# A pair's weighted sum as one group, and a shared two-bank tile, in an attention kernel with experts behind it

## The chip, the cores and the metric

The kernel runs on one core of one Trainium2 chip. The metric is the time of one execution on the device in microseconds (us); the time given for a kernel is the median of several runs. Both kernels compute the same outputs from the same inputs.

## What is computed

Causal attention with a learned decay, 4 batches of 8 heads, 576 positions of 64 features; then a layer of eight experts, of which each of the 2304 tokens uses one; then a dense layer with a squared ReLU. All in float32.

```python
scores = scale * np.matmul(q, k.transpose(0, 1, 3, 2))
cum = np.cumsum(np.maximum(s, 0.0), axis=-1)
bias = -(cum[:, :, :, None] - cum[:, :, None, :])
scores = np.where(causal, -1000000000.0, scores + np.minimum(bias, 0.0))
attn = np.exp(scores - np.max(scores, axis=-1, keepdims=True))
attn = attn / (np.sum(attn, axis=-1, keepdims=True) + 1e-09)
out = np.matmul(attn, v)                      # 32 heads of 576 x 64
x = out as 2304 tokens x 512
e_idx = np.argmax(x @ w_gate, axis=1)         # one expert a token
out[mask] = gate_w[mask, None] * eom[mask, e, None] * (relu(x[mask] @ w1[e]) @ w2[e])
return np.square(relu(out @ w_in)) @ w_out
```

## The kernel before, in words

The program has three stages: attention, which fills the first quarter of the span together with the choice of experts; the experts; the dense layer. The change lies in attention and touches the border to the experts.

Attention works on 16 **pairs** of heads, four pairs to a batch. A pair's 576 rows are four blocks of 128 and a tail of 64. Its scores come in seven **units**: 0 and 1 are the first two blocks, each with both heads; 2, 3 and 10, 11 are the third and fourth block of the first and of the second head; 4 is the **tail**, the last 64 rows of both heads, 576 columns wide and thus two PSUM banks. The order of units is `[0, 1, 3, 11, 2, 10, 4]`. Every unit goes through the same steps: `emit_s` (line 636) computes scores on TensorE into PSUM; `emit_m` (line 663, VectorE) adds the mask while it reads PSUM and finds the row's maximum; `emit_e` (line 680, ScalarE) is the exponential; `emit_t` (line 696) transposes the result p on TensorE; `emit_v` (lines 715 and 717) copies the transposes to SBUF. Then the weighted sum: `emit_pv` (line 733) multiplies with v in two **halves**, half 0 the first 256 rows (two blocks of keys), half 1 the other 320 (five blocks); `emit_ov` (line 744) copies the result out of PSUM, `emit_rc` (lines 759 to 762) makes the reciprocals of the row sums, `emit_xt` and `emit_xe` (lines 771 and 806) transpose and scale the result, and `store_x` writes it to memory.

q and k of a coming pair are transposed on TensorE too (`qk_pe`, lines 549 and 551): part 0 is q, part 1 is k, part 2 the tails of both. `qk_hi` (line 576, ScalarE) writes the high part of each, and `qk_lo` (line 580, VectorE) the rest that the high part leaves, so that scores are made of products of two parts. The first two pairs take four such products per score, the others two, with their decay terms loaded beside.

There are three sets of PSUM tiles in this stage: a ring of three one-bank tiles `s` for the scores of the units other than the tail and for `emit_xt`; a ring of three one-bank tiles `t`; and one tile `s2` of two banks for the tail's scores. The ring `t` holds the transposes of p, those of q and k, and the weighted sums (there is no ring of their own, since `O=0`), and some steps of the gate's logits. A tile is taken in turn; whoever takes it waits until the tile's earlier readers are done.

The order of the work is a sorted list. Each step is entered with a time of its own by `at(key, fn)`, in units of which a pair has seven, and the list is then written out in the order of the keys, each engine getting its steps in that order. The keys come from the table `K_`: `pv` (a half's blocks), `ov`, `rc`, `xt`, `xe`, `sx` (behind the half), `qk`, `qkh`, `qkl` (transposes, high, low), `lt` (logits). The q and k of most pairs are made one frame early (`early`):

```python
def early(pp):
    return min(NU, 3 * max(pp - ND, 0))
```

After the last pair a first piece of expert work runs, whose products are `early_h` (line 1071) and `early_y` (line 1099). `x_hi` and `x_lo` (lines 1341 and 1347) then bring the first chunk's tokens from PSUM to the tile `xt`, and `emit_h` (line 1431) starts the experts' first products with it.

## Time and profile before

| what | value |
|---|---|
| median of three runs | 861.39 us (860.45 to 861.93) |
| profiled execution, its own time | 862.74 us |
| its span | 861.0 us |
| mean granted clock of TensorE in it | 0.998 of full speed |
| TensorE busy | 843.1 us, 98% of the span |
| VectorE, ScalarE, GpSimd busy | 60%, 53%, 30% |

The time of an execution is a little longer than its span, which runs from the first to the last instruction that the profiler records. Times in rows are microseconds from the span's start. PE is TensorE's matmul, PEld its weight load, DVE is VectorE, ACT is ScalarE, POOL is GpSimd. `t<-ident,qk` is an instruction that writes tile `t` from `ident` and `qk`; a float32 matmul or transpose leaves more than one record where it needs more than one pass. In brackets stands the idle time before an instruction and what ended it.

### The profile page before, as it was taken

What the parts mean: (1) busy time and instruction counts of PE and PEld (TensorE: products, weight loads), DVE (VectorE), ACT (ScalarE), POOL (GpSimd) and SP (SyncE); (2) the same over time, 40 slices, a digit from 0 to 9 for tenths busy, and PEclk for the clock granted to TensorE, in tenths of its full rate; (3) what the DMA queues carried; (4) which work ended last, traced back from release to release, by engine and by line L of the source; (5) the groups of instructions that cost most, each with busy time, mean ns of one, the idle gap of its engine ahead of it and who ended that gap; (6) DMA issues with size and microseconds to landing.
All of it is one profiled execution on the core that took longest, in us unless ns stands there. A gap on an engine that the chain in (4) does not pass through costs nothing.

```text
span 861.0 us, 15161 instructions
## 1 busy us (share of the span) xinstructions
PE 843.1 (98%) x5412; PEld 748.7 (87%) x5412; DVE 520.4 (60%) x1180; ACT 452.3 (53%) x1012; POOL 262.1 (30%) x304
## 2 busy tenths in 40 slices
PE   8999999999999999999999999999999999999995
PEld 6876777777799999999999999999999999999994
DVE  7667777978777677768976767664233343232221
ACT  7787878988465446566655545443233232233221
POOL 6322334543126465566422232331101011001001
PEclk9999999999999999999999999999999999999999
DMA  7676677753287898999983433321010121001001
GB/s 168 137 162 142 144 183 180 178 127 91 78 278 232 255 252 266 233 280 274 296 246 96 147 120 101 100 84 62 13 62 37 37 75 38 1 1 37 1 0 40
DMA packets 113029, 113.14 MB, mean 131 GB/s; under 512 B 66034, under 2 KB 83954, under 8 KB 112947
## 3 DMA queue, kind: packets, MB, share of 16 engines
q1 hardware_dynamic: 104962, 96.68, 42.1%
q0 software_dynamic: 3664, 9.62, 3.3%
q10 hardware_dynamic: 4320, 5.80, 2.0%
q8 instruction: 45, 0.74, 0.4%
q14 instruction: 38, 0.30, 0.1%
HBM read 80.50 MB, written 23.32 MB: 121 GB/s over the span
## 4 chain that ended last, share of the span: by engine, by line
PE 47%; issue 31%; DVE 6%; ACT 6%; POOL 5%; DMA 4%; POOLq 1%; SPq 0%; ACTq 0%; DVEq 0%
PE z L1431 14%; PE z L1482 7%; PE z L1473 6%; PE s L636 5%; PE t L733 5%; PE t L696 4%; DMA cv<-in_moe_w_out_dram 2%; ACT p L680 2%; POOL out_dram L1541 1%; DVE w L250 1%; POOL cvm L1400 1%; PE t L549 1%; POOL cvm L1399 1%; ACT sta L576 1%; DMA w_out_d<-cvm 1%
## 5 line engine op out<-in xcount | busy, mean ns | idle before, releaser
L1431 PE MATMUL z<-xt,w 128*128 128x384 f32 (+6 forms) x1920 | 329.7, 320 | 0.7 <-DVE h L1442 0.6
L1431 PEld LDWEIGHTS z<-xt,w 128*128 128x128 f32 x1920 | 308.1, 188 | 9.8 <-DVE h L1442 1.2
L1482 PE MATMUL z<-w,h 128*128 128x512 f32 x864 | 214.9, 393 | 0.0
L1482 PEld LDWEIGHTS z<-w,h 128*128 128x128 f32 x864 | 160.7, 188 | 29.3
L1451 DVE SCALAR_TENSOR_TENSOR r<-z,r 128x384 f32<-128x384 f32 x96 | 53.3, 556 | 127.2 <-ACT r L1450 127.2
L1450 ACT ACTIVATE r<-z 128x384 f32<-128x384 f32 x96 | 47.2, 492 | 150.3 <-PE z L1431 149.3
L1473 PE MATMUL z<-h,w 128*128 128x304 f32 (+5 forms) x768 | 111.3, 294 | 0.4 <-DVE h L1442 0.2
L1473 PEld LDWEIGHTS z<-h,w 128*128 128x128 f32 x768 | 104.0, 189 | 1.2 <-ACT h L1441 0.4
L1399 POOL TENSOR_TENSOR cvm<-cvm,cva 128x512 f32<-128x512 f32 x32 | 43.5, 1361 | 170.6 <-DVE cva L1395 121.9
L1541 POOL DMA_INDIRECT out_dram<-ysb,tok_m x18 | 17.4, 969 | 245.5 <-ACT ysb L1528 183.2
L1458 DVE TENSOR_TENSOR h<-r,h 128x384 fp32r<-128x384 f32 x96 | 61.0, 636 | 50.3 <-ACT h L1457 49.7
L680 ACT ACTIVATE p<-p,nm 128x128 f32<-128x128 f32 (+3 forms) x144 | 84.3, 590 | 3.7 <-DVE nm L663 2.3
L1457 ACT CAST h<-r 128x384 fp32r<-128x384 f32 x96 | 49.3, 513 | 64.1 <-DVE r L1451 63.8
L250 DVE TENSOR_TENSOR w<-stg,w 128x1024 fp32r<-128x1024 f32 x49 | 75.1, 1534 | 5.4 <-ACT w L246 5.4
L663 DVE CUSTOM_DVE_ANT_0 p<-s,mask 128x128 f32<-128x128 f32 (+3 forms) x128 | 59.7, 486 | 30.4 <-PE s L636 29.3
L696 PE MATMUL t<-ident,p 128*128 128x128 f32 x400 | 69.1, 283 | 2.8 <-DVE sta L580 1.1
L246 ACT CAST w<-stg 128x1024 fp32r<-128x1024 f32 x49 | 51.4, 1049 | 22.0 <-POOL cvm L1400 18.2
L696 PEld LDWEIGHTS t<-ident,p 128*128 128x128 f32 x400 | 44.4, 140 | 18.7 <-ACT p L680 6.2
L597 POOL CAST stb<-sta 64x1152 fp32r<-64x1152 f32 x28 | 31.4, 1150 | 79.7 <-PE s L636 46.3
L1400 POOL TENSOR_TENSOR cvm<-cvs,cvm 128x512 f32<-128x512 f32 x32 | 54.2, 1694 | 2.5
L636 PE MATMUL s<-sta 128*64 128x288 f32 (+4 forms) x204 | 50.0, 342 | 0.9 <-DVE sta L580 0.9
L715 ACT COPY pt<-t 128x512 f32<-128x512 f32 (+1 forms) x94 | 47.0, 515 | 7.3 <-PE t L733 4.1
(242 smaller groups left out, 1024.8 us busy)
## 6 DMA issues: line engine op xcount, KB each, us to landing
stg<-in_moe_w_dram SPq DMA_DIRECT2D x42, 512.0 KB
cv<-in_moe_w_out_dram SPq DMA_DIRECT2D x16, 512.0 KB
stx<-in_moe_w_dram SPq DMA_DIRECT2D x14, 512.0 KB
cv<-in_moe_w_in_dram SPq DMA_DIRECT2D x14, 512.0 KB
xr<-yT_d SPq DMA_DIRECT2D x8, 768.0 KB
qk<-in_q_dram SPq DMA_DIRECT2D x32, 128.0 KB
v<-in_v_dram SPq DMA_DIRECT2D x32, 128.0 KB
stg<-in_moe_w_dram SPq DMA_DIRECT2D x16, 256.0 KB
```

What stands on the lines that cost most here:

```text
L250: nc.vector.tensor_tensor(out=lo, in0=raw.pop(job), in1=hi.bitcast(F32), op=ALU.subtract)
L636: nc.tensor.matmul(ps[0:mw, d0:d0 + nn], lhsT=ql[r, m0:m0 + mw], rhs=kl[r, c0:c0 + nn], start=(i == 0 and (tail or n == 0)), stop=(done an ...
L663: nc.vector.tensor_tensor_reduce(out=dst, in0=src, in1=msk, scale=-1.0, scalar=3.0e38, op0=ALU.add, op1=ALU.min, accum_out=nm[:, c:c + 1])
L680: nc.scalar.activation(out=pt[:, cs], in_=pt[:, cs], func=AF.Exp, scale=-1.0, bias=nm[:, c:c + 1], accum_out=rs[:, r:r + 1])
L696: nc.tensor.transpose(tp[:, i * P:(i + 1) * P], pt[:, j0:j0 + P], ident)
L1399: nc.gpsimd.tensor_tensor(out=m, in0=m, in1=a.bitcast(F32), op=ALU.mult)
L1400: nc.gpsimd.tensor_tensor(out=m, in0=sq, in1=m, op=ALU.add)
L1431: nc.tensor.matmul(ps[:, 0:n], lhsT=wa[:, zw, kk, fl * P:(fl + 1) * P], rhs=xt[:, zx, kk, 0:n], start=(i == 0), stop=(i == 3 * KD - 1))
L1451: nc.vector.scalar_tensor_tensor(out=gg, in0=ps[:, 0:TT], scalar=0.0, in1=gg, op0=ALU.max, op1=ALU.mult)
L1458: nc.vector.tensor_tensor(out=ht[:, 1], in0=gg, in1=ht[:, 0].bitcast(F32), op=ALU.subtract)
L1473: nc.tensor.matmul(y_acc[g][d][:, 0:n], lhsT=wb[:, zw, fl, d * P:(d + 1) * P], rhs=ht[:, zh, 0:n], start=(f == 0 and i == 0), stop=(f == n ...
L1482: nc.tensor.matmul(acc, lhsT=ht[:, zh, c * P:(c + 1) * P], rhs=wb[:, zw, fl, :], start=(first and i == 0), stop=(last and i == 2))
```

## The change

Five things are done together.

- The transposes of q and of k (parts 0 and 1) go into the two banks of one `s2` tile, for every pair from the third on but one (the fourth, which stays in ring `t`): thirteen pairs. Part 2 stays in ring `t`.
- The weighted sum of a pair is one group: half 0 moves to directly before half 1, both into the two banks of one `s2` tile. The last pair keeps its two groups and ring `t`.
- The transposed p of units 0 and 1 has two buffers instead of one, each laid out without a gap (768 floats a partition and pair instead of 1024), and its copies are contiguous.
- The reciprocals of both halves are made in one step.
- Keys: transposes of q and k at `qk2`, later by 0.95, 0.56 and 0.30; the rest of half 0 at `x0`; `sx` and one `lt`.

```diff
     wz=1.0,
     ring=['o', 't', 'o', 'o', 't', 's'],
     go=7.15,
-    lt=[[-0.37, -0.33, 0.07, 0.12], [-0.22, 0.14, 0.64, 0.96]],
+    lt=[[-0.37, -0.33, 0.07, 0.12], [-0.36, 0.14, 0.64, 0.96]],
     ltact=[1, 1],
     ptb=1,
     order=[0, 1, 3, 11, 2, 10, 4],
@@ -54,18 +54,20 @@
...
     sck=-5.35,
     qk=[-3.45, -2.16, -1.89],
+    qk2=[-2.5, -1.6, -1.59],
     qkh=0.61,
     qkl=0.65,
     dup=-2.9,
     dupa=0.6,
-    pv=[[3.74, 3.87], [8.47, 8.49, 8.51, 8.53, 8.57]],
+    x0=10.87,
+    pv=[[8.45, 8.46], [8.47, 8.49, 8.51, 8.53, 8.57]],
     ovact=[1, 1],
     gk=[4.59, 4.65, 5.02, 5.22, 5.65, 6.55, 7.35, 7.38, 7.54, 8.68, 9.78, 10.48, 10.95, 11.72, 12.72, 14.11, 14.46, 14.36, 14.48, 14.97, 15.87, 16.25, 17.18, 17.4, 19.12, 20.76],
...
     xe=1.32,
-    sx=2.42,
+    sx=3.9,
     w0=6.88,
     wld=2.9,
...
             cum_k = apool.tile([P, S], F32R, name="cum_k")
             cum_q = cq_p.tile([P, 2 * ND, S], F32R, tag="cq", name="cum_q")
-            pt0 = [apool.tile([P, 2, 2, 256], F32, name=f"pt0{a}") for a in range(K_["ptb"])]
+            pt0 = [apool.tile([P, 2, 3 * P], F32, name=f"pt0{a}") for a in range(2)]
             pt1 = [apool.tile([P, 2, NB, S - 256], F32, name=f"pt1{a}") for a in range(K_["ptb"])]
 
             def bank(r):
@@ -499,6 +501,8 @@
                 for _ in range(n):
                     nc.tensor.matmul(wt[:, 0:w], lhsT=onesb, rhs=onesb.unsqueeze(1).to_broadcast([P, w // P, P]), start=True, stop=True)
...
             qk_ps = {}
 
+            def early(pp):
+                return min(NU, 3 * max(pp - ND, 0))
+
+            def in_s2(pp):
+                return pp >= ND and early(pp) != 3
+
             def qk_pe(pp, part):
-                ps = qk_ps[pp, part] = bank(K_["ring"][part])
+                if part < 2 and in_s2(pp):
+                    if part == 0:
+                        qk_ps[pp] = ps_2.tile([P, 1024], F32, tag="s2", name="s2")
+                    ps = qk_ps[pp][:, 512 * part:512 * part + 512]
+                else:
+                    ps = bank(K_["ring"][part])
+                qk_ps[pp, part] = ps
                 if part < 2:
                     t = raw_q[pp][:, part * QM:(part + 1) * QM]
                     for c in range(NB - 1):
@@ -701,8 +717,8 @@
                 j0 = 0
                 for i, (tp, n) in enumerate(t_t.pop((pp, u))):
                     if u < 2:
-                        src = tp[:, 0:n * P].rearrange("p (h j i) -> p h j i", h=2, i=P)
-                        dst = pt0[pb][:, :, 0:u + 1, u * P:(u + 1) * P]
+                        src = tp[:, 0:n * P].rearrange("p (h c) -> p h c", h=2)
+                        dst = pt0[pp % 2][:, :, u * P:(2 * u + 1) * P]
                     elif u == NB - 1:
                         src = tp[:, 0:n * P].rearrange("p (j h i) -> p h j i", h=2, i=TAIL)
                         dst = pt1[pb][:, :, j0:j0 + n, S - TAIL - 256:S - 256]
@@ -721,19 +737,27 @@
             def emit_pv(pp, half, jbs):
                 vt = raw_v[pp]
                 if jbs[0] == 0:
-                    o_t[pp, half] = ps_o.tile([P, 512], F32, tag=o_tag, name=o_tag)
+                    if pp == NPAIR - 1:
+                        o_t[pp, half] = ps_o.tile([P, 512], F32, tag=o_tag, name=o_tag)
+                    else:
+                        if half == 0:
+                            o_t[pp] = ps_2.tile([P, 1024], F32, tag="s2", name="s2")
+                        o_t[pp, half] = o_t[pp][:, 512 * half:512 * half + 512]
                 o = o_t[pp, half]
                 last = 1 if half == 0 else NB - 1
-                pt = (pt0 if half == 0 else pt1)[pp % K_["ptb"]]
                 n = 256 if half == 0 else S - 256
                 base = 0 if half == 0 else 2
                 for jb in jbs:
                     c0 = max(jb - base, 0) * P
+                    if half == 0:
+                        pt = pt0[pp % 2][:, :, 2 * c0:n + c0]
+                    else:
+                        pt = pt1[pp % K_["ptb"]][:, :, jb, c0:n]
                     for hd in range(2):
                         nc.tensor.matmul(
                             o[64 * hd:64 * hd + 64, c0:n],
                             lhsT=vt[:, jb, hd, :],
-                            rhs=pt[:, hd, jb, c0:n],
+                            rhs=pt[:, hd],
                             start=(jb == 0), stop=(jb == last))
 
             def emit_ov(pp, half, act):
@@ -754,7 +778,7 @@
                 b, j = divmod(pp, HP)
                 rc = rc_t[pp] = rc_all[b % 2][:, 2 * j:2 * j + 2]
                 rsv = rs.rearrange("p (h t) -> p h t", h=2)
-                b0, b1 = (0, 2) if half == 0 else (2, NB)
+                b0, b1 = (0, 2) if half == 0 else (2 if pp == NPAIR - 1 else 0, NB)
                 if half == 1:
                     nc.vector.tensor_copy(out=rs[0:TAIL, 2 * NB - 1:2 * NB], in_=rs[P - TAIL:P, NB - 1:NB])
                 nc.vector.tensor_scalar(
@@ -1231,12 +1255,7 @@
             new_half(wpool1, (0, "a"), "w0")
             new_half(wpool1, (0, "b"), "w1")
 
-            order = K_["order"]
-            NU = len(order)
             at(NU * ND + 0.5, init_spare)
-
-            def early(pp):
...
                 base = NU * pp
@@ -1250,12 +1269,12 @@
                     else:
                         at(K_["od"][0], scale_tail, pp, nc.vector)
                     for part in range(3):
-                        tq = t0 + K_["qk"][part] - early(pp) + (0 if pp >= ND else K_["q1"])
+                        tq = t0 + K_["qk2" if in_s2(pp) else "qk"][part] - early(pp) + (0 if pp >= ND else K_["q1"])
                         at(tq, qk_pe, pp, part)
                         at(tq + K_["qkh"], qk_hi, pp, part)
                         at(tq + K_["qkl"], qk_lo, pp, part)
                 if pp >= ND:
-                    tb = t0 + max(K_["dup"], K_["qk"][2] + K_["qkl"] - early(pp) + 0.4)
+                    tb = t0 + max(K_["dup"], K_["qk2" if in_s2(pp) else "qk"][2] + K_["qkl"] - early(pp) + 0.4)
...
                     at(tb - 0.04, copy_b, pp)
...
                     tx = tv + K_["xe"]
                     at(tv + K_["ov"], emit_ov, pp, half, K_["ovact"][half])
-                    at(tv + K_["rc"], emit_rc, pp, half)
+                    if end or half == 1:
+                        at(tv + K_["rc"], emit_rc, pp, half)
+                    if not end and half == 0:
+                        tv = tv - K_["pv"][0][-1] + K_["x0"]
+                        tx = tv + K_["xe"]
                     at(tv + K_["xt"], emit_xt, pp, half)
                     if end:
                         at(tx, emit_xl, pp, half)
```

The rows below show what this moves on the engines. A row is one instruction or several alike: line, operation, what it writes and reads, its size, and the engines or DMA queues that it waits for.

TensorE behind the tail's scores of the third pair, before; the last row of the tail's scores stands first:

```order
L636 MATMUL s_865<-sta_137 64x288 x4
L549 MATMUL t<-ident,qk 128x128 [waits DMAHW3_49,DMAHW2_49,PE_49]
L549 MATMUL t<-ident,qk 128x128 x3
L733 MATMUL t<-pt_154,v_142 64x256 [waits DMAHW5_49,Activation_49]
L733 MATMUL t<-pt_154,v_142 64x256 [waits DMAHW6_49]
L733 MATMUL t<-pt_154,v_142 64x128 x2
L696 MATMUL t<-ident,p 128x128 [waits Activation_49]
L696 MATMUL t<-ident,p 128x128 x2
L636 MATMUL s<-sta_135 128x192 [waits DMAHW0_49,DVE_49,Pool_49]
L636 MATMUL s<-sta_135 128x192 [waits DMAHW7_49]
L636 MATMUL s<-stb_139 128x192 x2
L549 MATMUL t<-ident,qk 128x128 [waits DMAHW6_49,DMAHW5_49,Activation_49]
```

TensorE at the same place, changed; here `s_892` is an `s2` tile, and the tail's scores end three rows above the first row:

```order
L652 MATMUL s<-sta_135 128x192 [waits DMAHW0_49,DVE_49,Pool_49]
L652 MATMUL s<-sta_135 128x192 [waits DMAHW7_49]
L652 MATMUL s<-stb_139 128x192 [waits DMAHW5_49]
L652 MATMUL s<-stb_139 128x192 [waits DMAHW6_49]
L565 MATMUL s_892<-ident,qk 128x128 [waits DMAHW3_49,DMAHW2_49,DVE_49]
L565 MATMUL s_892<-ident,qk 128x128 x3
L795 MATMUL s<-ident,oT_310 128x128 x2
L712 MATMUL t<-ident,p 128x128 [waits Activation_49]
L712 MATMUL t<-ident,p 128x128 x2
L652 MATMUL s<-sta_135 128x256 x2
L652 MATMUL s<-stb_139 128x256 x2
L565 MATMUL s_892<-ident,qk 128x128 [waits DVE_49]
```

The weighted sum of half 0 (line 733) is gone from here; the q transposes, which were first, stand behind the scores of the next unit (192 wide), and the k transposes, which stood there, behind those of the unit after it (256 wide); both now wait for VectorE.

ScalarE from the last exponentials of the third pair on, before:

```order
L680 ACTIVATE p,rs_156<-p,nm 128x384 [waits DVE_49]
L576 ACTIVATE sta_137<-t 128x512 [waits DMAHW1_49,DMAHW0_49,PE_49]
L744 COPY oTx<-t 128x256 [waits PE_49]
L680 ACTIVATE p,rs_156<-p,nm 128x576 [waits DVE_49]
L576 ACTIVATE sta_137<-t 128x512 [waits DMAHW1_49,PE_49,Pool_49]
L715 COPY pt_155<-t 128x3x128 [waits PE_49]
L576 ACTIVATE sta_137<-t 128x2x64 [waits PE_49]
L680 ACTIVATE p,rs_157<-p,nm 128x128 [waits DVE_49,Activation_49]
L680 ACTIVATE p,rs_157<-p,nm 128x128 [waits DVE_49]
L715 COPY pt_155<-t 128x2x3x64 [waits PE_49]
L715 COPY pt_155<-t 128x2x2x64 [waits PE_49]
```

ScalarE at the same place, changed:

```order
L696 ACTIVATE p,rs_157<-p,nm 128x384 [waits DVE_49,Activation_49]
L696 ACTIVATE p,rs_157<-p,nm 128x576 [waits DVE_49]
L592 ACTIVATE sta_137<-s_892 128x512 [waits DMAHW1_49,DMAHW0_49,PE_49]
L731 COPY pt_156<-t 128x3x128 [waits PE_49]
L696 ACTIVATE p,rs_158<-p,nm 128x128 [waits DVE_49] x2
L592 ACTIVATE sta_137<-s_892 128x512 [waits DMAHW1_49,DVE_49,PE_49]
L592 ACTIVATE sta_137<-t 128x2x64 [waits PE_49]
L731 COPY pt_156<-t 128x2x3x64 [waits PE_49]
L731 COPY pt_156<-t 128x2x2x64 [waits PE_49]
L696 ACTIVATE p,rs_158<-p,nm 128x256 [waits DVE_49,Activation_49]
L696 ACTIVATE p,rs_158<-p,nm 128x256 [waits DVE_49]
```

The exponential of the tail (576 wide) moved from behind q's high part to ahead of it; the copy of a weighted sum (`oTx`) is gone from here; k's high part (the second row of 512) moved behind the copy of a transpose and two exponentials.

ScalarE at the end of attention, before, where `sta_136` holds the early expert work and `xt` the first chunk's tokens:

```order
L1088 CAST sta_136<-z_3600 128x512 [waits PE_49]
L1077 ACTIVATE qk<-z_3577 128x512 [waits PE_49]
L1088 CAST sta_136<-z_3653 128x512 [waits PE_49]
L1341 CAST xt<-z_3659 128x4x128 [waits PE_49,Activation_49,Pool_49]
L1341 CAST xt<-z_3690 128x4x96 [waits PE_49]
L1586 COPY ysb<-z_3646 128x512 [waits DMAHW5_49,DMAHW6_49,DMAHW1_49,DMAHW7_49,DMAHW0_49,PE_49]
```

ScalarE at the same place, changed:

```order
L1112 CAST sta_136<-z_3543 128x512 [waits DMAHW5_49,PE_49]
L1101 ACTIVATE qk<-z_3520 128x512 [waits PE_49]
L1112 CAST sta_136<-z_3596 128x512 [waits PE_49]
L1364 CAST xt<-z_3602 128x4x128 [waits DMAHW0_49,DVE_49,DMAHW5_49,PE_49,DMAHW7_49,Activation_49,Pool_49]
L1364 CAST xt<-z_3633 128x4x96
L1609 COPY ysb<-z_3589 128x512 [waits DMAHW6_49,DMAHW5_49,DMAHW7_49,DMAHW1_49,DMAHW0_49]
```

The first cast of `xt` has got four waits more, on VectorE and three DMA queues, the second cast has lost its own, and the copy `ysb` behind them no longer waits for TensorE.

## Rows read from the trace of the kernel before

**Rows 1.** The page's busy time, share of the span and instructions of each engine.
```profile
PE 843.1 (98%) x5412; PEld 748.7 (87%) x5412; DVE 520.4 (60%) x1180; ACT 452.3 (53%) x1012; POOL 262.1 (30%) x304
```

**Rows 2.** Windows: us, then PE, PEld, DVE, ACT, POOL busy, PEclk, DMA share, GB/s.
```profile
40.00:80.00 40.00, 38.81 (x310) 29.72 (x308) 28.24 (x99) 31.96 (x93) 10.80 (x14) 1.00 0.70 158
...
400.00:800.00 400.00, 399.79 (x2166) 367.31 (x2165) 205.23 (x320) 160.70 (x296) 78.52 (x74) 1.00 0.29 91
```

**Rows 3.** TensorE's timeline, 50 to 63 us: start, us, engine, line, operation, idle before.
```profile
50.53 0.60 PE L549 MATMUL t<-ident,qk 128*128 128x128 f32 x4
51.06 0.87 PE L733 MATMUL t<-pt,v 128*64 128x256 f32 x8
51.86 0.55 PE L696 MATMUL t<-ident,p 128*128 128x128 f32 x3
...
52.67 0.60 PE L549 MATMUL t<-ident,qk 128*128 128x128 f32 x4
53.11 0.38 PE L771 MATMUL s<-ident,oTx 128*128 128x128 f32 x2
...
54.39 0.79 PE L696 MATMUL t<-ident,p 128*128 128x128 f32 x5
...
56.47 0.92 PE L696 MATMUL t<-ident,p 128*128 128x128 f32 x4 [0.16 <-ACT p L680]
...
57.68 2.27 PE L733 MATMUL t<-pt,v 128*64 128x320 f32 x20
59.89 0.66 PE L696 MATMUL t<-ident,p 128*128 128x128 f32 x4
...
62.56 0.60 PE L549 MATMUL t<-ident,qk 128*128 128x128 f32 x4
```

**Rows 4.** VectorE's timeline, the same stretch.
```profile
51.52 0.08 DVE L663 DVE_READ_ACCUMULATOR2_ANT nm<- 128x1 f32 x1
51.85 0.69 DVE L580 SCALAR_TENSOR_TENSOR sta<-t,sta 128x512 fp32r<-128x512 f32 x1 [0.25 <-issue]
```

**Rows 5.** ScalarE's timeline, the same stretch.
```profile
51.16 0.60 ACT L576 ACTIVATE sta<-t 128x512 fp32r<-128x512 f32 x1 [0.30 <-PE t L549]
...
52.24 0.78 ACT L680 ACTIVATE p<-p,nm 128x576 f32<-128x576 f32 x1
...
53.36 0.60 ACT L576 ACTIVATE sta<-t 128x512 fp32r<-128x512 f32 x1 [0.24 <-POOL sta L598]
53.86 0.48 ACT L715 COPY pt<-t 128x384 f32<-128x384 f32 x1
54.23 0.28 ACT L576 ACTIVATE sta<-t 128x128 fp32r<-128x128 f32 x1
...
55.17 0.75 ACT L715 COPY pt<-t 128x384 f32<-128x384 f32 x2
...
56.70 0.21 ACT L680 ACTIVATION_READ_ACCUMULATOR p<-p,nm 128x1 f32 x1
```

**Rows 6.** VectorE's timeline in a frame with gate logits.
```profile
128.11 0.55 DVE L858 TENSOR_TENSOR lw<-t,rca 128x384 f32<-128x384 f32 x1
...
129.44 0.70 DVE L580 SCALAR_TENSOR_TENSOR sta<-t,sta 128x512 fp32r<-128x512 f32 x1
```

**Rows 7.** Waits of TensorE's weight loads, 36 to 212 us: us, times, longest.
```profile
PEld t L696 <- DVE sta L580: 3.5, 9, 1.0
```

**Rows 8.** TensorE's timeline where attention ends and expert work begins.
```profile
236.08 1.17 PE L1099 MATMUL z<-w,sta 128*128 128x512 f32 x4
237.08 1.50 PE L1431 MATMUL z<-xt,w 128*128 128x224 f32 x12
```

**Rows 9.** ScalarE's timeline at the same place.
```profile
232.50 0.59 ACT L1341 CAST xt<-z 128x512 fp32r<-128x512 f32 x1
234.13 0.48 ACT L1341 CAST xt<-z 128x384 fp32r<-128x384 f32 x1 [1.05 <-PE z L333]
```

More of the change, by code (lines that the diff above doesn't have):

```diff
@@ L500, in warm @@
                     nc.tensor.matmul(wt[:, 0:w], lhsT=onesb, rhs=onesb.unsqueeze(1).to_broadcast([P, w // P, P]), start=True, stop=True)
+            order = K_["order"]
+            NU = len(order)
             raw_q = {}
@@ L1232, in attention_moe_ffn_kernel @@
             new_half(wpool1, (0, "b"), "w1")
-            order = K_["order"]
-            NU = len(order)
             at(NU * ND + 0.5, init_spare)
-            def early(pp):
-                return min(NU, 3 * max(pp - ND, 0))
             for pp in range(NPAIR):
```

## The prediction, made before the changed kernel was run

> **What bounds the kernel now.** I read the page's busy shares first, then the windows by stage, then TensorE's timeline over one turn of the attention loop, and beside it VectorE's and ScalarE's. The page shows TensorE busy for 98% of the span, and no other engine above 60% [rows 1]. The windows say where the rest lies: from 400 to 800 us TensorE is busy for 399.79 of 400 us, so what reaches that stage late ends late by as much; from 40 to 80 us it is busy for 38.81 of 40 [rows 2]. The granted clock is 1.00, the upper level of 2.4 GHz, in both. So the change is decided in the attention loop and at its end, and every microsecond lost there is a microsecond of the total.
>
> In the loop one pair takes 62.56 - 50.53 = 12.03 us from one q transpose behind the tail's scores to the next [rows 3]. The reader is to see that this is a tight chain between three engines, not TensorE's own work alone: the group at 56.47 sits idle 0.16 us for an exponential, although the busy share hides this. The tail's scores, two banks wide, are read by VectorE until 51.52 + 0.08 = 51.60 [rows 4]. ScalarE is almost without a gap [rows 5]; before, it evicts q (51.16) while VectorE still masks the tail.
>
> **Part by part: PV in one group.** I work out the fixed price of a group from two groups of the same kind. Half 0 is eight records with 1536 columns in all and holds TensorE from 51.06 to 51.86, 0.80 us; half 1 is twenty records with 4864 columns and holds it from 57.68 to 59.89, 2.21 us [rows 3]. The slope is 1.41/3328 us a column, which leaves 0.80 - 0.65 = 0.15 us that is no column's. Ahead of PV, four transposes take 51.06 - 50.53 = 0.53 us, and ahead of other full-width work 53.11 - 52.67 = 0.44 us [rows 3]; so a group's entry costs 0.09. Together 0.24 us a group, and merging fifteen pairs would save 15 x 0.24 = 3.6 us if TensorE were the only limit. The Trainium skill, "TensorEngine Tiling (Array Packing)", Key Properties, says that changing the tiling mode drains TensorE; by that rule alone the sum would be these -3.6 us, and the rows agree with a price of that kind.
>
> Against it stands where half 0 now is. It moves from behind the q transposes to directly ahead of half 1, so its 0.65 us lies behind the last thing half 1 waits for. The normalisers of both halves become one step: two small VectorE operations a pair go, off the path, so I cost that at nothing; VectorE's cover, 60% busy [rows 1], would leave at most their own length if gone.
>
> **q and k in the shared tile.** This is the term that decides. The tail's scores, the q and k transposes and PV now take one two-bank tile in turn, with no second buffer. From the order of the changed program: the first q transpose waits for VectorE's reading of the tail's scores; the first k transpose waits again for VectorE, which I take for the low part of q, since the tile is guarded as a whole. ScalarE's order now has the tail's exponential ahead of q's high part. The chain of one turn, counted from the end of the tail's scores (50.53):
> mask read 1.07 [rows 4]; hop between engines 0.09 (51.76, the end of q's high part [rows 5], to 51.85 [rows 4]); tail's exponential 0.78; q high 0.60 [rows 5]; hop 0.09; q low 0.69 [rows 4]; hop 0.09; four k transposes 0.60 [rows 3]; hop 0.09; k high 53.36 to 53.86, 0.50; the tails' high part 54.23 to 54.40, 0.17; two copies of the tail and two exponentials of unit 1, 55.17 to 56.70 + 0.21 = 56.91, 1.74 [rows 5]; from there to PV 57.68, 0.77; half 0 in the group 0.65; and from 57.68 to the end of the next tail's scores 62.56, 4.88 [rows 3].
> The sum is 12.81 us, against 12.03: +0.78 a turn. Unit 10's copy (53.86 to 54.23, 0.37) and the two exponentials of unit 0 (54.40 to 55.17, 0.77 [rows 5]) are on ScalarE too, but they fit into the 0.09 + 0.69 + 0.09 + 0.60 + 0.09 = 1.56 us in which it waits for q's low part and the k transposes; if that cover is gone, up to 1.14 comes back. The four hops may be hidden in part; without any the chain is 12.45, +0.42. The lower bound is thus +0.42, the upper about +1.2 (below); I take +0.78, the value with every row at its own length.
>
> How many turns: thirteen pairs have q and k in the tile. Two of these run in the first frames, whose scores take four passes instead of two, so TensorE has longer work there and hides the chain. 11 x 0.78 = +8.6 us.
>
> In the three frames that also make a batch's gate logits, VectorE has 129.44 - 128.11 = 1.33 us of product and sum between the tail's mask and q's low part [rows 6]. The price lies between 0 and 1.33 a frame. Before, transposes already waited 3.5 us in nine waits for VectorE's low parts [rows 7], so part of it is paid already, and in a plain turn VectorE has the slack of tail's exponential and q's high part, 1.38 less its own copy and masks. I take 0.4, the low side: +1.2 us. The four merged groups outside those eleven turns gain 4 x 0.24 = -1.0 us.
>
> The Trainium skill, "Perfetto Trace Analysis", section Matmuls under Optimizing Tensor Performance, speaks against the change: independent matmul groups should rotate through different PSUM banks, so that the eviction of one overlaps the next group's matmuls. Here three groups that did so are put into one tile; no row of the kernel before shows that tile shared, and by the rule the sign is that of my sum.
>
> **The hand-off to the experts.** Before, the first chunk's two ScalarE casts run at 232.50 and 234.13 [rows 9], long before the last early products (from 236.08), and the first expert matmul starts at 237.08 behind that product without a gap [rows 8]. In the order of the change, the first cast has a longer list of waits and the copy behind it has lost its wait for TensorE, which fits a cast that now waits for the last early product: the exponentials' transposed tile has grown and the memory laid out behind it has shifted. Then both casts, 0.59 + 0.48 [rows 9], stand between the products' end (236.08 + 1.17 = 237.25) and the first expert matmul: 237.25 + 1.07 = 238.32, +1.2 us. Bounds: 0 (if the wait is older), and 2.2 (if the low part, of similar length on VectorE, must follow). I take 1.2, since the first matmuls need only the high part. Expert work is bound by TensorE, so it is not won back.
>
> **Sum:** 8.6 + 1.2 - 1.0 + 1.2 = +10.0 us on the profiled execution's 862.74, which is 872.7; the median of the three runs shown, 861.39, lies 1.35 below that execution, so the forecast of the median is 871.4. The reorder of other copies between buffers, the later store of x and the earlier logit step I cost at nothing: the x products keep their place behind the tail's scores, and the store's readers are a batch away. If the store were late, logits would wait instead, which is inside the 0.4's bound. The clock stays: it is granted in full through the loop with its present waits [rows 2], and the new ones, some 0.4 us each, are no longer than the longest of 1.0 there [rows 7].
>
> **The rivals.**
> *TensorE stays the bound (faster).* The drains saved are then all that counts, with the hand-off: 862.74 - 3.6 + 1.2 - 1.35 = 859.0. It decides at the k transposes: TensorE's other work up to them, 0.81 (51.86 to 52.67) + 0.35 of wait + 0.53 + 1.28, brings it there some 2.97 us after the tail's scores, and q's low part ends at 3.32 by the chain. Were that 0.35 earlier and ScalarE not late behind it, nothing would be held. For it speaks the 98% of [rows 1]; against it the gapless ScalarE [rows 5]. Chance 0.05.
> *The halves are guarded one by one (slower, less).* If the wait of the first k transpose is for an older reading, q's low part is off the path: 1.07 + 0.09 + 0.78 + 0.50 + 0.37 + 0.77 + 0.50 + 0.17 + 1.74 + 0.77 + 0.65 + 4.88 = 12.29, +0.26 a turn; 11 x 0.26 = 2.9, with -1.0 and +1.2: 864.5. Against it speaks that the order shows a wait for VectorE where there was one for ScalarE. Chance 0.08.
> *ScalarE has no room (slower, more).* If unit 0's masks, behind a copy on VectorE, come so late that its exponentials don't fit the 1.56 us, about 0.4 more stands in each turn: 11 x 1.2 = 13.2, and 13.2 + 1.2 - 1.0 + 1.2 = 14.6: 876.0. Chance 0.12.
> *The waits only take the place of old ones (no change).* The new waits would fall into idle time that each turn already has, and drains saved and hand-off about cancel: 861.4 give or take 1.5. Against it: the new chain is longer than the whole turn. Chance 0.03.
>
> **How the numbers follow.** My forecast has 0.72. A change can be told from none at about 0.2%, 1.7 us. Faster 0.05 (the first rival), same 0.03 (the last), slower 0.92 (the others). The range runs from 866.0, which takes in the chain without most of its hops (872.7 - 11 x 0.36 = 868.7, less 1.35 and less the logits' 1.2: 866.2), to 877.0, which takes in the crowded ScalarE; it leaves out 0.05 + 0.03 + 0.08 below and a few hundredths above.
>
> **What would show it.** A plain turn of about 12.8 us between tails' scores; TensorE waiting for VectorE at line 565 twice a turn, about 0.35 us before q and as much or more before k; waits of the p transposes for VectorE's low parts (3.5 us before) nearly gone; PV half 0 directly ahead of half 1; the first expert cast starting after the last early product and the first expert matmul about 1.1 us behind its end. I am wrong if the turn stays at 12.0 or falls below, if line 565 does not wait for VectorE, or if the loss appears behind 240 us.

## The result, and the profile after

| | before | changed |
|---|---|---|
| median | 861.22 us (860.45 to 861.93, 4 runs) | 872.11 us (871.62 to 872.61, 4 runs) |
| profiled execution, its span | 862.74 us, 861.0 us | 872.42 us, 870.7 us |

The ratio is 1.0124, with a 95% interval of 1.0109 to 1.0139: 10.9 us slower. The forecast was 871.4, in a range of 866.0 to 877.0.

The page's busy row, against [rows 1]:

```profile
PE 839.3 (96%) x5412; PEld 747.2 (86%) x5412; DVE 511.7 (59%) x1150; ACT 449.5 (52%) x1012; POOL 264.0 (30%) x304
```

TensorE does the same 5412 matmuls and weight loads, but is busy for 96% of a longer span. TensorE's timeline over two turns, with the columns of [rows 3] (L565 are q's and k's transposes, L757 is the weighted sum, L712 the transposes of p; the tail's scores end at 50.94 and 63.71):

```profile
52.07 0.66 PE L565 MATMUL s<-ident,qk 128*128 128x128 f32 x4 [0.21 <-DVE nm L679]
...
54.23 0.66 PE L565 MATMUL s<-ident,qk 128*128 128x128 f32 x4 [0.49 <-DVE sta L596]
...
58.09 2.92 PE L757 MATMUL s<-pt,v 128*64 128x256 f32 x28
60.95 0.66 PE L712 MATMUL t<-ident,p 128*128 128x128 f32 x4
...
63.71 0.49 PE L712 MATMUL t<-ident,p 128*128 128x128 f32 x3
...
64.84 0.66 PE L565 MATMUL s<-ident,qk 128*128 128x128 f32 x4 [0.21 <-DVE nm L679]
...
67.01 0.66 PE L565 MATMUL s<-ident,qk 128*128 128x128 f32 x4 [0.49 <-DVE sta L596]
...
70.86 2.92 PE L757 MATMUL s<-pt,v 128*64 128x256 f32 x28
```

A turn lasts 70.86 - 58.09 = 12.77 us, 12.03 before. Twice in each TensorE sits idle at line 565, 0.21 us for the mask's reading and 0.49 us for q's low part; all its idle time in a turn is 0.86 us, 0.21 before. The one group takes 60.95 - 58.09 = 2.86 us where the two took 0.80 + 2.21. VectorE and then ScalarE in the first of these turns, against [rows 4, 5]:

```profile
51.93 0.08 DVE L679 DVE_READ_ACCUMULATOR2_ANT nm<- 128x1 f32 x1
...
53.49 0.69 DVE L596 SCALAR_TENSOR_TENSOR sta<-s,sta 128x512 fp32r<-128x512 f32 x1 [0.59 <-POOL stb L613]
```

```profile
52.05 0.78 ACT L696 ACTIVATE p<-p,nm 128x576 f32<-128x576 f32 x1 [0.77 <-DVE nm L679]
...
52.82 0.58 ACT L592 ACTIVATE sta<-s 128x512 fp32r<-128x512 f32 x1
...
54.93 0.60 ACT L592 ACTIVATE sta<-s 128x512 fp32r<-128x512 f32 x1 [0.37 <-PE s L565]
...
55.58 0.76 ACT L731 COPY pt<-t 128x384 f32<-128x384 f32 x2
```

The chain reads from row to row: mask read until 52.01 (1.07 behind the tail's scores), exponential 52.05, q high 52.82, q low 53.49 to 54.18, k's transposes 54.23, k high 54.93, the tail's copies 55.58. TensorE's waits from 36 to 222 us (us in total, times, longest):

```profile
PE s L565 <- DVE sta L596: 10.1, 12, 1.9
PE s L652 <- DMA sta<-aug_d: 1.5, 1, 1.5
PE s L565 <- DVE nm L679: 1.3, 6, 0.2
```

At the end of attention, TensorE and then ScalarE, against [rows 8, 9] (L335 brings in gathered tokens, L1123 are the early products, L1454 the first expert's, L1364 the casts):

```profile
241.03 0.66 PE L335 MATMUL z<-ident,xr 128*128 128x128 f32 x4 [0.69 <-DMA xr<-x_d,tbl_i]
...
245.40 1.18 PE L1123 MATMUL z<-w,sta 128*128 128x512 f32 x4
247.75 1.60 PE L1454 MATMUL z<-xt,w 128*128 128x224 f32 x12 [1.18 <-ACT xt L1364]
```

```profile
246.73 0.97 ACT L1364 CAST xt<-z 128x512 fp32r<-128x512 f32 x2 [5.77 <-PE z L1123]
```

The last transposes of the early expert work, before and then changed:

```profile
231.35 0.60 PE L1082 MATMUL z<-ident,qk 128*128 128x128 f32 x4
```

```profile
239.74 0.60 PE L1106 MATMUL z<-ident,qk 128*128 128x128 f32 x4
```

Along the program the loss builds up so. These transposes start 8.39 us later, which is attention's part. Behind the gather's wait of 0.69 the last early product starts 9.32 us later (245.40 against 236.08). At the hand-off 1.35 more is lost: the first expert product starts 2.35 us behind that early product where it was 1.00 before, 1.18 of it idle time; so it stands at +10.67 (247.75 against 237.08). Behind it some comes back: the first product of the dense layer starts at 465.86 against 456.35, +9.51, and the spans differ by 9.7. TensorE's idle time at the first experts' products was 1.0 us before, in four waits for VectorE and ScalarE, and is 0.2 now, the hand-off aside; that is most of the return.

### The profile page after: what moved, and what is told of

Its sections match the earlier page's. It is cut to its first block, busy times and chain, and to the rows that moved or that the text cites. A ratio compares the mean times of both kernels' runs of the same rounds, so it can differ in the third digit from the quotient of the medians.

```text
span 870.7 us, 15105 instructions
## 1 busy us (share of the span) xinstructions
PE 839.3 (96%) x5412; PEld 747.2 (86%) x5412; DVE 511.7 (59%) x1150; ACT 449.5 (52%) x1012; POOL 264.0 (30%) x304
## 4 chain that ended last, share of the span: by engine, by line
PE 54%; issue 30%; DVE 5%; ACT 5%; POOL 2%; DMA 1%; POOLq 1%; SPq 1%; DVEq 0%; ACTq 0%
PE z L1454 19%; PE z L1496 11%; PE z L1505 7%; PE s L757 5%; PE s L652 4%; PE t L712 3%; ACT p L696 2%; POOL out_dram L1564 1%; DVE p L679 1%; DVE sta L596 1%; ACT sta L592 1%; PE z L335 1%; PE s L565 1%; PE s L795 1%; ACT pt L731 1%
## 5 line engine op out<-in xcount | busy, mean ns | idle before, releaser
L1454 PE MATMUL z<-xt,w 128*128 128x384 f32 (+6 forms) x1920 | 329.7, 320 | 1.3 <-ACT xt L1364 1.2
L1454 PEld LDWEIGHTS z<-xt,w 128*128 128x128 f32 x1920 | 308.0, 188 | 10.5 <-ACT xt L1364 1.6
L252 DVE TENSOR_TENSOR w<-stg,w 128x1024 fp32r<-128x1024 f32 x49 | 73.0, 1489 | 4.5 <-ACT w L248 4.5
L712 PE MATMUL t<-ident,p 128*128 128x128 f32 x400 | 66.4, 280 | 2.0 <-ACT p L696 0.4
L712 PEld LDWEIGHTS t<-ident,p 128*128 128x128 f32 x400 | 45.3, 141 | 14.5 <-ACT pt L731 6.2
```

The lines of the kernel that those rows point to most:

```text
L252: nc.vector.tensor_tensor(out=lo, in0=raw.pop(job), in1=hi.bitcast(F32), op=ALU.subtract)
L712: nc.tensor.transpose(tp[:, i * P:(i + 1) * P], pt[:, j0:j0 + P], ident)
L1454: nc.tensor.matmul(ps[:, 0:n], lhsT=wa[:, zw, kk, fl * P:(fl + 1) * P], rhs=xt[:, zx, kk, 0:n], start=(i == 0), stop=(i == 3 * KD - 1))
```

## The experiments

Two theories stood against each other at first. Theory 1: q, k and half 0 form one chain, each part alone costs little. Theory 2: each part has a price of its own. Ratios are to the kernel before, with 95% intervals.

**e1_k_ring.** k's transposes go back to the ring.

```diff
-                if part < 2 and in_s2(pp):
+                if part < 1 and in_s2(pp):
```

> The change with one thing undone: the transposes of k go back to the ring t, at the changed program's place in the order; those of q and both halves of the weighted sum stay in the shared tile. Theory 1 (the second wait, of k's transposes for q's low part, is the price): that wait, 10.1 us of idle TensorE at line 565 in the changed kernel, is gone, a plain turn falls from 12.77 to about 12.3 us (0.49 us less), and the time to about 866.5. Theory 2 (the late place of q and k behind the tail's mask is the price, and the wait only shows it): k's transposes come a little earlier but ScalarE has copies and exponentials ahead of k's high part, and they take a tile from the ring that the transposes of p want; the turn stays at 12.7 or above, and the time at 871 to 875.

Measured: 872.68 us, 1.0136 (1.0119 to 1.0153). TensorE's timeline of a turn:

```profile
65.22 0.66 PE L565 MATMUL s<-ident,qk 128*128 128x128 f32 x4 [0.22 <-DVE nm L679]
...
66.73 0.60 PE L565 MATMUL t<-ident,qk 128*128 128x128 f32 x4
...
68.78 0.44 PE L712 MATMUL t<-ident,p 128*128 128x128 f32 x2 [1.02 <-ACT pt L731]
...
71.39 0.87 PE L757 MATMUL s<-pt,v 128*64 128x256 f32 x8
```

The wait at line 565 for q's low part is gone, and k's transposes start 66.73 - 65.22 = 1.51 us behind q's, 67.01 - 64.84 = 2.17 in the changed kernel. But the idle time has moved: 1.02 us at the transposes of p, whose tile in the ring waits for ScalarE's copy. A turn is 12.92 (groups at 58.47 and 71.39). Theory 1's lower time did not come; taking the wait away by way of the crowded ring gains nothing.

**e2_pv_only.** The weighted sum alone.

```diff
-                return pp >= ND and early(pp) != 3
+                return False
```

> One part of the change alone: the weighted sum as one group in the shared tile, with all that goes with it (the two compact buffers, one step for the reciprocals); q and k are transposed into the ring t at the keys of the kernel before. Theory 1 (one chain: half 0 costs only because the q and k chain ends ahead of it): TensorE works on through the tail's mask, half 0 is only moved, fifteen drains of 0.24 us are saved, the hand-off costs 1.2: a plain turn of 11.8 to 12.0 us and 859 to 862 us in all. Theory 2 (each part has a price of its own): half 0 no longer fills the place behind the tail's scores where TensorE waits, so the transposes of p wait there for ScalarE instead; a turn of about 12.4, and 865 to 868 us.

Measured: 868.51 us, 1.0083 (1.0066 to 1.0100). The time is a little above theory 2's range. A plain turn, though, is 12.10 (groups at 57.15 and 69.25), just above theory 1's 11.8 to 12.0; it is the frames with the gate's work that lose, such as 96.18 to 109.45, 13.27 against 12.58 before. The waits of the weight loads and of the matmuls from 36 to 222 us, and TensorE in that frame:

```profile
PEld t L712 <- DVE sta L596: 12.8, 22, 1.4
PE t L712 <- DVE sta L596: 7.1, 15, 1.2
```

```profile
104.66 0.55 PE L712 MATMUL t<-ident,p 128*128 128x128 f32 x3 [0.85 <-DVE sta L596]
```

The weight loads of the transposes of p now wait 12.8 us for the ring's tiles, which VectorE's low part of q or k still holds; before it was 3.5 us in nine waits [rows 7]. Of this TensorE itself sits idle for 7.1 us, 1.1 before. Theory 2 had named ScalarE there; it is VectorE.

**e3_qk_only.** q and k alone, on the kernel before.

```diff
+                if part < 2 and in_s2(pp):
+                    if part == 0:
+                        qk_ps[pp] = ps_2.tile([P, 1024], F32, tag="s2", name="s2")
+                    ps = qk_ps[pp][:, 512 * part:512 * part + 512]
...
-                        tq = t0 + K_["qk"][part] - early(pp) + (0 if pp >= ND else K_["q1"])
+                        tq = t0 + K_["qk2" if in_s2(pp) else "qk"][part] - early(pp) + (0 if pp >= ND else K_["q1"])
```

> The other part alone, made from the kernel before: q and k of the thirteen pairs in the shared tile at the changed keys; the weighted sums, their buffers and the reciprocals as before, in two groups in the ring t. The hand-off is as before. Theory 1 (one chain): the chain of 12.81 less half 0's 0.65 is 12.16 a turn, 0.13 over the turn of before: 862 to 863 us. Theory 2 (each part has a price of its own): both waits stay at line 565, half 0 fills a part of them, and the turn is about 12.4: 865 to 868 us.

Measured: 867.22 us, 1.0065 (1.0048 to 1.0081). TensorE's timeline of a turn (L749 is the weighted sum):

```profile
57.95 2.27 PE L749 MATMUL t<-pt,v 128*64 128x320 f32 x20
...
62.92 0.87 PE L749 MATMUL t<-pt,v 128*64 128x256 f32 x8
...
64.54 0.60 PE L565 MATMUL s<-ident,qk 128*128 128x128 f32 x4
...
66.61 0.66 PE L565 MATMUL s<-ident,qk 128*128 128x128 f32 x4 [0.44 <-DVE sta L596]
...
70.47 1.84 PE L749 MATMUL t<-pt,v 128*64 128x320 f32 x12
```

A turn is 70.47 - 57.95 = 12.52, not the 12.16 of theory 1. Half 0 stands ahead of q's transposes here (62.92), so these start 1.62 us behind the tail's scores instead of 1.13, and k's still wait 0.44 us. Taking half 0 out of the end of the chain puts most of it in at the start. So e3 loses 6 and e2 7, e2 with the hand-off's 1.35 in it, and theory 1 falls in its strong form. In the traces the two parts nearly add up: the last transposes of the early expert work start at 235.12 in e2 and at 236.85 in e3, 3.77 and 5.50 later than before, together 9.27, where the change has 8.39.

**e4_handoff.** Another pool for the two buffers.

```diff
+            pt0_p = actx.enter_context(tc.tile_pool(name="pt0_p", bufs=1))
...
-            pt0 = [apool.tile([P, 2, 3 * P], F32, name=f"pt0{a}") for a in range(2)]
+            pt0 = [pt0_p.tile([P, 2, 3 * P], F32, name=f"pt0{a}") for a in range(2)]
```

> The change with another memory layout alone: the two buffers of the transposed p of units 0 and 1 lie in a pool of their own at the same place, so that the first chunk's tile no longer falls on the pool that the early expert work uses; its casts then wait for the same things as in the kernel before. Theory 1 (the hand-off loses the 1.18 us that TensorE sits idle ahead of line 1454): the first expert product starts without a gap and the time falls by 1.0 to 1.3, to about 871.0. Rival (something else is late there, such as the gather of tokens or the weights): the gap stays under another name, and the time stays within 0.4 of 872.1.

Measured: 871.30 us, 1.0119 (1.0102 to 1.0136). By time this is not told apart from the change (0.8 us less); by trace it is. TensorE's first expert product:

```profile
246.31 1.50 PE L1455 MATMUL z<-xt,w 128*128 128x224 f32 x12
```

It starts without idle time, 1.00 us behind the last early product (245.31) as before, 2.35 in the changed kernel, and the first cast runs at 241.73, ahead of that product. So the hand-off costs 1.35. This execution did not wait for the gather either, but was 0.84 later at the end of attention, so the starts themselves (246.31 and 247.75) are not to be compared. The edit moves nothing but the border between two pools, and with it the wait goes: the cast waited because of what else lay in the pool under its tile.

**e5_halves and e7_qk_halves.** The shared tile as two one-bank tiles, for the change and for e3. The tail's mask becomes two steps. For e7, half 0 and half 1 stay in the ring.

```diff
-                        qk_ps[pp] = ps_2.tile([P, 1024], F32, tag="s2", name="s2")
+                    ps = bank2(part)
...
+            def bank2(z):
+                return ps_2.tile([P, 512], F32, tag="s2" + "ab"[z], name="s2" + "ab"[z])
...
-                    ps = ps_2.tile([P, 1024], F32, tag="s2", name="s2")
+                    ps = [bank2(0), bank2(1)]
...
+                    jobs = [(pt[:, z * w:(z + 1) * w], sv[z], mask_t[:, z * w:(z + 1) * w], z) for z in range(2)]
...
+                        out=dst, in0=src, in1=msk, scale=-1.0, scalar=nm[:, 0:1] if u == NB - 1 and c else 3.0e38, op0=ALU.add, op1=ALU.min,
```

> The changed kernel with its shared two-bank tile made into two one-bank tiles, each guarded by itself: the tail's scores fill both, their mask is read in two steps of 288 columns, the second going on from the first one's maximum; q and half 0 use the first tile, k and half 1 the second. Theory 1 (the transposes of k wait for q's low part only because the tile is guarded as a whole): the wait of line 565 for VectorE's low part, 10.1 us in the changed kernel, is gone; a plain turn falls from 12.77 to about 12.3 us and the time by 4 to 6, to 866 to 868 us. Theory 2 (ScalarE, with the tail's exponential ahead of q's high part, is what is late, and k's wait only stands ahead of the next one): the idle time moves to the transposes of p behind k, the turn stays at 12.6 or more, and the time at 870 to 872.

> Only q and k moved (the earlier run of the kernel before with q and k alone in the shared tile, 867.2 us), with the tile made into two one-bank tiles as in e5_halves; weighted sums as before. Theory 1 (the guard of the whole tile makes q's and k's part of the price): the 0.45 us ahead of k's transposes in each plain turn go, a turn falls from 12.52 to about 12.1, and the time to 862 to 864 us. Theory 2 (the late place of q and k): the turn stays at 12.4 or more, 866 us or more.

Measured: e5 865.42 us, 1.0051 (1.0035 to 1.0067); e7 863.77 us, 1.0025 (1.0015 to 1.0035). TensorE's timeline of a turn of e5 (`s2a`, `s2b` are the two tiles), then of e7:

```profile
58.49 0.87 PE L759 MATMUL s2a<-pt,v 128*64 128x256 f32 x8
...
64.77 0.60 PE L567 MATMUL s2a<-ident,qk 128*128 128x128 f32 x4
...
66.23 0.60 PE L567 MATMUL s2b<-ident,qk 128*128 128x128 f32 x4
...
68.85 0.44 PE L716 MATMUL t<-ident,p 128*128 128x128 f32 x2 [0.89 <-ACT pt L735]
...
70.83 0.87 PE L759 MATMUL s2a<-pt,v 128*64 128x256 f32 x8
```

```profile
58.34 2.27 PE L753 MATMUL t<-pt,v 128*64 128x320 f32 x20
...
64.92 0.60 PE L567 MATMUL s2a<-ident,qk 128*128 128x128 f32 x4
...
66.39 0.60 PE L567 MATMUL s2b<-ident,qk 128*128 128x128 f32 x4
...
70.42 2.27 PE L753 MATMUL t<-pt,v 128*64 128x320 f32 x20
```

VectorE's low part of q in the same turn of e5:

```profile
66.73 0.69 DVE L598 SCALAR_TENSOR_TENSOR sta<-s2a,sta 128x512 fp32r<-128x512 f32 x1 [0.65 <-POOL sta L616]
```

k's transposes come 1.46 us behind q's in e5, 2.17 in the changed kernel, and wait for nothing: they start at 66.23, ahead of q's low part (66.73), for which they had to wait while both lay in one tile. A turn falls to 12.34 in e5 and to 12.08 in e7. Two tiles for one are thus worth 872.11 - 865.42 = 6.7 us in the change and 867.22 - 863.77 = 3.5 in e3; this holds the earlier start of q's transposes too, which wait for the first half of the mask alone (in e5 they start 0.75 us behind the tail's scores, 1.13 in the changed kernel). The ten executions of e5 lie between 863.25 and 870.12, so its 6.7 is rough. In e5 some idle time comes back at the transposes of p (0.89 us), now for ScalarE's copy: the next link. What e7 still loses, 2.5 us, is not in its plain turns (12.08 against 12.03) but in frames that carry steps of the gate as well: two of them grew by 0.85 and 0.81 (groups at 109.61 and 122.48, 162.23 and 175.07), with a like wait of 0.89 for ScalarE's copy.

**e6_reciprocals and e8_half1_s2.** Two parts of the change that the prediction costs at nothing, each on the kernel before.

```diff
-                b0, b1 = (0, 2) if half == 0 else (2, NB)
+                b0, b1 = (0, 2) if half == 0 else (2 if pp == NPAIR - 1 else 0, NB)
...
+                    if end or half == 1:
+                        at(tv + K_["rc"], emit_rc, pp, half)
+                    if not end and half == 0:
+                        tv = base + 10.87
+                        tx = tv + K_["xe"]
```

```diff
+                    if half == 0 or pp == NPAIR - 1:
+                        o_t[pp, half] = ps_o.tile([P, 512], F32, tag=o_tag, name=o_tag)
+                    else:
+                        o_t[pp, half] = ps_2.tile([P, 1024], F32, tag="s2", name="s2")
```

> The kernel before with the parts of the change that use no tile of PSUM otherwise: one step for the reciprocals of both halves, half 0's transposes back and scaling later, behind it, with the changed keys x0, sx and lt. The prediction costs these at nothing: within 1 us of the kernel before, no loss. Rival (the later end of a pair delays the store, the logits or the gate): 2 us or more over it. A gain of about 1 would say that VectorE's two small operations, or the place of half 0's transposes, were on the path.

> The kernel before with one edit: half 1 of the weighted sum writes the two-bank tile instead of a tile of the ring t, in its place in the order; half 0 and all else stay. Theory 1 (the price of the weighted sum's part is half 0's move away from behind the tail's scores, where it gave VectorE and ScalarE time): nothing changes, 860.5 to 862.5 us. Theory 2 (the tail's scores now wait for the weighted sum's copy, so the shared tile itself costs): the tail's scores come late and the time is 864 us or more.

Measured: e6 860.67 us, 0.9992 (0.9982 to 1.0003); e8 861.12 us, 0.9998 (0.9989 to 1.0007). Neither costs anything that can be told. What is left of e2's price beside the hand-off is half 0's move, with its second buffer and compact copies, which were not tried by themselves.

**e9_later and e10_mended.** A try at a faster version, and the change with both costs mended.

```diff
-    sck=-5.35,
+    sck=-5.6,
-    xe=1.32,
+    xe=1.44,
-                        tv = base + 10.87
+                        tv = base + 11.0
```

These three lines are e9's on top of e6; e10 has the edits of e4 and of e5 together.

> A try at a version that beats the kernel before: the merged reciprocals of e6_reciprocals on the kernel before, with half 0's transposes back a little later still (11.0 in place of 10.87), the scaling behind them later (xe 1.44 in place of 1.32) and the tail's scaling earlier (sck -5.6 in place of -5.35). If what e6_reciprocals gained (0.6 us, inside its interval) is real and comes from VectorE's steps leaving the place behind the tail's scores, this should give 0.8 to 1.5 us: 859.8 to 860.5. If it was noise, 861.2.

> The change with both of its named costs mended: the shared tile as two one-bank tiles (e5_halves, 865.4 us) and the pool of their own for the buffers of the transposed p (e4_handoff). What is left is the move of half 0 and the late place of q and k. If the hand-off's price is its 1.18 us of idle TensorE and adds to the rest, 864.2 to 864.7, still 3 us above the kernel before; if e5_halves has hidden it, 865.4 again.

Measured: e9 860.30 us, 0.9992 (0.9984 to 1.0001), which the interval does not tell from the kernel before. e10 864.72 us, 1.0041 (1.0028 to 1.0055). TensorE of e10 at the hand-off:

```profile
241.10 1.18 PE L1126 MATMUL z<-w,sta 128*128 128x512 f32 x4
242.12 1.49 PE L1457 MATMUL z<-xt,w 128*128 128x224 f32 x12
```

The gap is gone there too; that the 0.7 us between e5 and e10 are its worth is not shown by their intervals. No version that clearly beats the kernel before was found.

## Why the prediction was right

- **The bound.** TensorE stays at its limit behind attention: from 400 to 800 us it is busy for 400.00 us, so nothing lost in attention was won back there. The granted clock is 1.00 there and from 40 to 80 us, as forecast.
- **The turn.** Forecast 12.81, measured 12.77. The links agree one by one: mask read 1.07 behind the tail's scores, one group 2.86 (0.65 + 2.21), q's low part 0.09 behind its high part. The allowance for hops was a little large: k's transposes start 3.29 us behind the tail's scores, not 3.41; from the group to the end of the next tail's scores it is 5.62 in place of 0.65 + 4.88 = 5.53, and the two nearly cancel. ScalarE had the room that one rival denied it: it sat idle for 0.37 us ahead of k's high part (54.93).
- **The guard of the whole tile.** Taken from the order alone, shown by e5 and e7. The rival with halves guarded one by one gave 12.29 a turn and 864.5 us; e5 built that case, with the mask in two steps besides, and gave 12.34 and 865.42. The Trainium skill, "Perfetto Trace Analysis", section Matmuls under Optimizing Tensor Performance, asks that independent groups rotate through different PSUM banks; the runs agree, with 6.7 us between one tile and two. Its gain appears only where the tiles, not only the banks, are separate: the changed kernel already wrote q and k to different banks.
- **Terms that were mis-sized.** That the sum for attention, 8.6 + 1.2 - 1.0 = 8.8, met 8.39 is in part luck: two misses nearly cancel. The eleven turns were to cost 8.6 + 1.2 = 9.8 and cost 8.27 (half 1 of the second pair starts 0.38 later than before, half 1 of the thirteenth 8.65). The eight without logits kept to the chain, 0.80 each on average, from 0.37 to 1.56. The +1.2 for the three logit frames was about 0: they grew by 0.69, 0.53 and 0.68 us, no more than a plain turn's 0.74. VectorE did come late there, for k's transposes waited 1.14 us and not 0.49, but TensorE's own work in such a frame was shorter too (13.53 us without idle time, 13.94 before); why is not shown. The -1.0 for the groups outside these turns did not come either: all frames outside them together changed by 8.39 - 8.27 = +0.12. The whole sum, +10.0, was for profiled executions; these differ by 9.7, the medians by 10.9.
- **The first frames.** In the second frame of the changed kernel the scores waited 1.5 us for a load of decay terms. This is no cost of the change that the runs show: the frame before it had ended earlier, so that the second pair's half 1 starts only 0.38 later in all, and e6, with q, k and the weighted sums as before, has such a wait too (1.06 us).
- **The largest frame.** One frame with the gate's work grew by 1.56 (groups at 152.49 and 166.80 against 147.41 and 160.16). VectorE's gate steps stand ahead of q's low part, and k's transposes waited 1.94 us:

```profile
162.86 0.66 PE L565 MATMUL s<-ident,qk 128*128 128x128 f32 x4 [1.94 <-DVE sta L596]
```

- **Half 0.** The prediction put its price into the chain's end. e2 shows a second way in which it costs, without q and k in the tile: the waits for the ring fit that its 0.80 us behind the tail's scores gave VectorE time to free the tiles. By e6 and e8 neither the reciprocals nor half 1's place in the shared tile costs; the second buffer and the compact copies are not told apart from the move. The step "half 0's 0.65 us lies behind the last thing half 1 waits for" is right for the change, but was not all of the price.
- **The drains.** The group's fixed price is real: 2.86 us against 3.01 for the two, the 0.15 of the prediction; its 0.09 for the entry was not seen by itself. The Trainium skill, "TensorEngine Tiling (Array Packing)", Key Properties, on drains at a change of mode, fits that; no run turned it into a gain.
- **The hand-off.** Forecast +1.2, measured 1.35 from product to product, 1.18 of it idle, and e4 shows that the layout is its cause. The gather's wait of 0.69, which e4 did not have, and what came back behind the first expert product (10.67 there, 9.7 at the end) were not foreseen and nearly cancel.

## What to carry to other kernels

Before a tile of PSUM is shared, write down the chain that its readers and writers then form over one turn of the loop, row by row, and compare it with the turn: if it is longer, the busy share of the bound engine says nothing about the gain. Here a guard covered a tile, not the bank that is written, so two halves of one tile were in series where two tiles overlapped. And a step of the bound engine that could stand anywhere in its list may be what gives another engine time to free a buffer: when it moves, the bound engine waits there.

## What the runs showed of the hardware

VectorE's 16-bit step of the gate (line 969, 128x384) was stretched beside work on GpSimd. VectorE and then GpSimd in the frame that grew by 1.56 us:

```profile
157.45 0.54 DVE L969 TENSOR_SCALAR r<-iota_r,rk_all 128x384 bf16<-128x384 f16 x2
...
159.09 1.12 DVE L969 TENSOR_SCALAR r<-iota_r,rk_all 128x384 bf16<-128x384 f16 x1
...
161.02 1.18 DVE L969 TENSOR_SCALAR r<-iota_r,rk_all 128x384 bf16<-128x384 f16 x1
162.12 0.68 DVE L596 SCALAR_TENSOR_TENSOR sta<-s,sta 128x512 fp32r<-128x512 f32 x1
```

```profile
157.87 2.24 POOL L613 CAST stb<-sta 64x1152 fp32r<-64x1152 f32 x2 [4.04 <-PE s L652]
...
160.82 1.26 POOL L275 TENSOR_TENSOR w<-stg,w 128x512 fp32r<-128x512 f32 x1
```

Two such steps took 0.54 us together at 157.45, and one took 1.12 us (159.09) and 1.18 us (161.02). The long ones lie beside a cast or a subtraction on GpSimd (157.87 to 160.11, 160.82 to 162.08). All thirty such steps in the traces of the two kernels agree: the eighteen beside which GpSimd ran nothing took 0.29 to 0.31 us, the ten that lay beside its work for more than half of their length 0.53 to 1.21. That GpSimd is the cause is what the rows suggest; no run here took its work away. The second long step sits directly ahead of q's low part, and so on the new chain.
